# Two attention and two FFN layers on one core: FFN rows in homes of their own, spreads of 1/den by ScalarE and DMA

## The chip, the core and the metric
One core of one Trainium2 chip runs the whole program. The metric is the device time in microseconds of one launch. The engines are TensorE (PE in the rows, PEld for its weight loads), VectorE (DVE), ScalarE (ACT), GpSimd (POOL) and SyncE (SP), which here only issues DMAs.

## The reference
`x` has 2048 rows of 512 (bf16). Four residual layers follow each other, A, B, A, B, with the same weights both times (numbered L = 0 to 3):

```python
x = x + A(layernorm(x)); x = x + B(layernorm(x))   # twice
# A: 32 heads of 16
q, k, v = split(x @ wqkv)
phi = lambda t: where(t > 0, t + 1, exp(t)) + 1e-6
kv  = sum_s phi(k)[s] v[s]^T          # per head, 16 x 16
z   = sum_s phi(k)[s]
o   = (phi(q) @ kv) / (phi(q) . z + 1e-6)
A   = o @ wo
# B: 1792 hidden columns
B   = (silu(x @ w_gate) * (x @ w_up)) @ w_down
```

## The kernel before
The rows are 16 tiles of 128 (t), in 4 groups of 512 (g). The program is a list of tokens (`PROGRAM`, line 169) in the order in which TensorE does them; each token records its matmuls and all that belongs to it on the other engines. The order on the other four engines is written out by hand as well (`ORDER`, line 193), and `ON_ACT` (line 352) says which of two engines takes a step. Semaphore waits follow from the buffers that are read and written (`Prog.op`, `Prog.sync`). So a step runs when its turn has come on its engine and its inputs are there.

Tokens of an attention layer: `0k3` projects k of tile 3 and makes phi(k) (`k_proj`, line 663), `0g3` adds phi(k)^T x of tile 3 into four PSUM banks (`g_acc`; so kv is made from x first, and the weights of v come in later), `0z3` adds the sums z, `0q12` projects columns 2 of q for group 1 (`q_proj`), `0d12` makes the denominators of it (`den`, line 781), `0v` turns G into kv (`kvt`), `0m2` multiplies kv by Wo (`m_mm`), `0w5` is the output block of tile 5 with the residual (`wo`, line 854). The copies of G and of `0m` out of PSUM go to the buffer GT (`evac`, lines 741 and 744). `S` is a warming matmul on zeros.
Tokens of an FFN: `1u113` makes hidden columns 13 of group 1 (gate and up, `gu`, line 870), `1p25` is one of seven products of the down projection of group 2 (`down`, line 1101; a Winograd form of Strassen's scheme, so seven products instead of eight). In layer 3 some gate and up blocks are made by that scheme too (`3y...`, `gs`). `0t2` transposes a normed tile on TensorE (`xt_pe`, line 615).

`ln` (line 544) norms a tile: a sum (from the residual add, or for layer 0 by bn_stats on DVE or a copy with accumulation on ScalarE, line 564), a square with accumulation on ScalarE (line 572), variance and power -0.5 on DVE and POOL (lines 588, 592), and the apply on ScalarE (599) or DVE (603). Then SP transposes the tile by DMA into xnT (line 612), unless the token `t` does it. In attention layers the normed tile lies in xnA, one home per tile; in FFN layers in one of two buffers xnB that go round (line 553), and the square writes its unused output to one of three buffers etmp (line 568) that phi uses also.

1/den of a group has 32 numbers a row and has to be spread to 512. For 0d0, 0d1, 2d0 and 2d2 ScalarE takes a logarithm (line 797) and writes four spread tiles by an exponential (line 814) into one of two buffers rrep, SP transposes each, and DVE multiplies (line 832). For 0d3 and 2d3 DVE takes the reciprocal (803, 806) and ScalarE copies (819). For 0d2 and 2d1 (listed in `PE_T`) one exponential of 128 columns is transposed on DVE (808), TensorE spreads it by 16 small matmuls (`rep_pe`, line 834, token `0r2`), and DVE multiplies from PSUM (850).

## Time and profile before
| | us |
|---|---|
| median of 3 runs | 411.54 (411.19 to 414.91) |
| the profiled execution | 412.45 |
| its span | 410.5 |

The span is what the profile's rows cover; the execution's own time has 1.95 us around it. All times in rows are microseconds from the span's start. A group of rows names the line, the engine, the operation, the output and inputs, and the shape. In brackets stands how long the engine was idle before it and what ended that.

### The profile page before, as it was taken

What the parts mean: (1) busy time and instruction counts of PE and PEld (TensorE: products, weight loads), DVE (VectorE), ACT (ScalarE), POOL (GpSimd) and SP (SyncE); (2) the same over time, 40 slices, a digit from 0 to 9 for tenths busy, and PEclk for the clock granted to TensorE, in tenths of its full rate; (3) what the DMA queues carried; (4) which work ended last, traced back from release to release, by engine and by line L of the source; (5) the groups of instructions that cost most, each with busy time, mean ns of one, the idle gap of its engine ahead of it and who ended that gap; (6) DMA issues with size and microseconds to landing.
All of it is one profiled execution on the core that took longest, in us unless ns stands there. A gap on an engine that the chain in (4) does not pass through costs nothing.

```text
span 410.5 us, 7692 instructions
## 1 busy us (share of the span) xinstructions
PE 400.2 (97%) x2714; PEld 243.8 (59%) x2714; DVE 325.3 (79%) x754; ACT 245.9 (60%) x492; POOL 130.6 (32%) x277
## 2 busy tenths in 40 slices
...
PEclk9999999999999999999999999999999999999999
...
DMA packets 53190, 23.30 MB, mean 57 GB/s; under 512 B 46432, under 2 KB 52064, under 8 KB 53152
## 3 DMA queue, kind: packets, MB, share of 16 engines
...
q0 software_dynamic: 1344, 6.03, 4.6%
q10 hardware_dynamic: 544, 0.52, 0.4%
...
## 4 chain that ended last, share of the span: by engine, by line
PE 91%; DVE 4%; ACT 2%; DMA 1%; issue 1%; SPq 0%; DVEq 0%; ACTq 0%
PE pb L452 91%; DMA X<-in_A_x_dram 1%; DMA xnT<-xnB 1%; DVE X L862 1%; DVE pq L850 1%; DVE GT L744 0%; DVE pq L832 0%; ACT xnA L572 0%; ACT xnB L599 0%; ACT xnA L564 0%; DVE KVT L755 0%; DVE pq L659 0%; DVE pq L1205 0%; ACT xnT L631 0%; DVE etmp L652 0%
## 5 line engine op out<-in xcount | busy, mean ns | idle before, releaser
L452 PE MATMUL pb<-xnT,Wg 128*128 128x512 bf16 (+1 forms) x388 | 95.7, 363 | 1.4 <-issue 1.1
L452 PE MATMUL pb<-xnT,Wu 128*128 128x512 bf16 (+1 forms) x388 | 95.6, 363 | 0.0
L452 PEld LDWEIGHTS pb<-xnT,Wu 128*128 128x128 bf16 x388 | 37.9, 98 | 39.4
L452 PEld LDWEIGHTS pb<-xnT,Wg 128*128 128x128 bf16 x388 | 37.7, 98 | 36.1 <-issue 1.6
L896 DVE TENSOR_TENSOR hT<-tht,pb 128x512 bf16<-128x512 f32 x50 | 34.0, 682 | 22.0 <-PE pb L452 15.0
L894 ACT ACTIVATE tht<-pb 128x512 f32<-128x512 f32 x50 | 29.5, 592 | 27.9 <-PE pb L452 25.7
L647 ACT ACTIVATE etmp<-pb 128x512 bf16<-128x512 f32 x64 | 36.9, 597 | 12.1 <-PE pb L452 9.9
L1022 POOL TENSOR_TENSOR hT<-pq 128x256 bf16<-128x256 f32 x24 | 18.6, 778 | 77.2 <-ACT pq L1012 77.0
L576 POOL TENSOR_SCALAR mv<-sums 128x1 f32<-128x1 f32 x52 | 13.7, 271 | 87.4 <-DVE sums L1215 54.9
L885 ACT ACTIVATE tht<-pb 128x512 f32<-128x512 f32 x32 | 19.0, 595 | 35.5 <-PE pb L452 34.4
L452 PE MATMUL pb<-Wd,hT 128*128 128x256 bf16 x336 | 40.1, 273 | 0.0
L1027 ACT ACTIVATE pq<-pb 128x512 f32<-128x512 f32 x45 | 26.0, 595 | 22.6 <-PE pb L452 19.7
L592 POOL TENSOR_TENSOR rstd<-vpe,negh 128x1 f32<-128x1 f32 x62 | 35.9, 583 | 7.5 <-DVE sums L1215 2.7
L452 PEld LDWEIGHTS pb<-Wd,hT 128*128 128x128 bf16 x336 | 32.8, 98 | 5.8
L452 PE MATMUL pb<-Wqkv,xnT 128*128 128x512 bf16 x128 | 31.0, 379 | 2.4 <-ACT xnT L631 2.4
L1017 DVE TENSOR_TENSOR pq<-pb,pq 128x512 f32<-128x512 f32 x45 | 30.2, 684 | 3.6 <-PE pb L452 1.7
L452 PE MATMUL pb<-xnT,Wqkv 128*128 128x512 bf16 x128 | 31.9, 379 | 0.0
L452 PE MATMUL pb<-GT,pq 128*128 128x512 bf16 x128 | 30.2, 379 | 1.4 <-ACT GT L741 1.4
L452 PE MATMUL pb<-pk,xnA 128*128 128x512 bf16 x128 | 31.1, 379 | 0.0
L652 DVE TENSOR_SCALAR etmp<-etmp 128x512 bf16<-128x512 bf16 x64 | 18.3, 289 | 14.4 <-ACT etmp L647 14.2
L887 DVE SCALAR_TENSOR_TENSOR tht<-tht,pb 128x512 f32<-128x512 f32 x32 | 21.8, 684 | 6.2 <-ACT tht L885 6.0
L572 ACT ACTIVATE etmp<-X,sums 128x512 bf16<-128x512 bf16 x32 | 22.8, 714 | 3.9 <-DVE X L862 3.6
...
## 6 DMA issues: line engine op xcount, KB each, us to landing
...
```

Of the source, the lines that this page charges most:

```text
L452: return op("pe", lambda e: e.matmul(o_ap, lhsT=lhsT, rhs=rhs, start=start, stop=stop, skip_group_check=skip), r=r, w=w, n=n)
L572: op("act", lambda a: a.activation(out=sq_ap, in_=X[:, t, :], func=ACT.Square, scale=-float(D), bias=sums[:, t:t + 1], accum_out=mv[:, t, ...
L592: op("pool", lambda p: p.tensor_tensor(out=rstd[:, t:t + 1], in0=vpe[:, t:t + 1], in1=negh[:], op=ALU.pow), r=[f"vp{t}", "negh"], w=[f"rs{ ...
L647: exps.append(op("act", lambda a: a.activation(out=etmp[e][:], in_=PB[pb], func=ACT.Exp), r=[f"pb{pb}"], w=[f"e{e}"], after=silus, kind="e ...
L652: op("dve", lambda v: v.tensor_scalar(out=etmp[e][:], in0=etmp[e][:], scalar1=1.0, scalar2=1e-6, op0=ALU.min, op1=ALU.add), r=[f"e{e}"], w ...
L885: op("act", lambda e: e.activation(out=tht[a][:], in_=PB[pg], func=ACT.Tanh, scale=0.5), r=[f"pb{pg}"], w=[f"th{a}"], kind="tanh")
L887: op("dve", lambda v: v.scalar_tensor_tensor(out=tht[a][:], in0=tht[a][:], scalar=1.0, in1=PB[pg], op0=ALU.add, op1=ALU.mult), r=[f"pb{pg} ...
L894: silus.append(op("act", lambda e: e.activation(out=tht[a][:], in_=PB[pg], func=ACT.Silu), r=[f"pb{pg}"], w=[f"th{a}"], after=exps, kind=" ...
L896: op("dve", lambda v: v.tensor_tensor(out=hT[h][:, j, :], in0=tht[a][:], in1=PB[pu], op=ALU.mult), r=[f"pb{pu}", f"th{a}"], w=hk, kind="h")
L1017: op("dve", lambda v: v.tensor_tensor(out=c, in0=PB[b], in1=c, op=ALU.add), r=[f"pb{b}", k], w=[k], kind="ca")
L1022: lambda e: e.tensor_tensor(out=hT[h][:, jj, o:o + 256], in0=c[:, 0:256], in1=c[:, 256:512], op=ALU.mult),
L1027: op("act", lambda e: e.activation(out=gs_tmp[3 * f + n], in_=PB[pb], func=ACT.Copy), r=pk_, w=[f"gt{3 * f + n}"], kind="cp")
```

## The change
1. FFN rows: the normed tile of layers 1 and 3 goes to its own home, `pk[t]` for tiles 0 to 11 and `xnA[t]` for 12 to 15, and the square writes there as well. The ring xnB is gone.
2. Spreads: `PE_T` loses 0d2 and 2d1; all eight groups are now made by ScalarE's logarithm and exponentials and by DMA, 0d3 and 2d3 too. The ring rrep has four buffers. The small matrices for `rep_pe`, which ScalarE made at the start, are gone. `PE_T` gains 2t7.
3. Loads: the x tile 2 goes out on ScalarE's queue, between the two loads of k's weights.
4. The last group's third output block: the sum X + bank is made behind product 5, and the block is closed from that bank behind product 7.
5. The token list, the orders of the four engines and `ON_ACT` are all new. 31 warming matmuls stand ahead of tile 0's transposes instead of 51, and none behind them, where three stood.

The code (of the tables one line is shown):

```diff
 PE_T = set("""
-0d2 0t0 0t1 0t2 0t3 2d1
+0t0 0t1 0t2 0t3 2t7
 """.split())
...
         xnA = sb("xnA", [P, T, D // 2], FP32)[:].bitcast(BF16)
-        NXB = 2
-        xnB = [sb("xnB", [P, D], BF16) for _ in range(NXB)]
         NXT = 4
...
         esel = sb("esel", [P, H, DH], BF16) if any(x[1] == "d" for x in PE_T) else None
-        rrep = [sb("rrep", [P, 512], BF16) for _ in range(2)]
+        rrep = [sb("rrep", [P, 512], BF16) for _ in range(4)]
         RT = [sb("RT", [P, NC, 512], BF16) for _ in range(2)]
...
         r_pq = Ring(NPQ)
-        r_xb = Ring(NXB)
         r_xt = Ring(NXT)
         r_den = Ring(2)
-        r_rrep = Ring(2)
+        r_rrep = Ring(4)
         r_RT = Ring(2)
...
         for t in range(TG):
-            dma("sp", X[:, t, :], x2d[t * P:(t + 1) * P, :], w=[f"x{t}"], kind="ldx")
+            dma("act" if t == 2 else "sp", X[:, t, :], x2d[t * P:(t + 1) * P, :], w=[f"x{t}"], kind="ldx")
         for c in range(2):
...
             xk = f"x{t}"
-            if L % 2 == 0:
-                b_ap, bk = xnA[:, t, :], f"xa{t}"
-            else:
-                b = r_xb.take(1)
-                b_ap, bk = xnB[b][:], f"xb{b}"
+
+            b_ap, bk = (pk[t], f"pk{t}") if L % 2 and t < 12 else (xnA[:, t, :], f"xa{t}")
             if L == 0 and f"0s{t}" not in ON_ACT:
...
                        r=[xk], w=[bk, f"sm{t}"], kind="stats")
-                if L % 2:
-                    e = r_e.take()
-                    sq_ap, sqk = etmp[e][:], f"e{e}"
-                else:
-                    sq_ap, sqk = b_ap, bk
-                op("act", lambda a: a.activation(out=sq_ap, in_=X[:, t, :],
+                op("act", lambda a: a.activation(out=b_ap, in_=X[:, t, :],
                                                  func=ACT.Square, scale=-float(D), bias=sums[:, t:t + 1],
                                                  accum_out=mv[:, t, 1:2]),
-                   r=[xk, f"sm{t}"], w=[sqk, f"ss{t}"], kind="sq")
+                   r=[xk, f"sm{t}"], w=[bk, f"ss{t}"], kind="sq")
                 op("pool", lambda p: p.tensor_scalar(out=mv[:, t, 0:1], in0=sums[:, t:t + 1], scalar1=-1.0 / D,
...
                    r=[xk, f"mv{t}", f"rs{t}"], w=[bk], kind="apply")
-            if L % 2 and f"{L}t{t}" not in PE_T:
-                r_xb.done(b)
-            xn_of[L, t] = b_ap, bk, None if L % 2 == 0 else b
+            xn_of[L, t] = b_ap, bk
             if f"{L}t{t}" not in PE_T:
...
             dst = xnT[sl][:, :, tl * P:(tl + 1) * P]
-            b_ap, bk, xb = xn_of[L, t]
-            if xb is not None:
-                r_xb.done(xb)
+            b_ap, bk = xn_of[L, t]
             pb = bank()
...
             alone = last or f"{L}o{g}" in ON_ACT
-            assert done.issuperset({2: (1,), 6: (1,), 7: (6,), 4: (7,), 3: (5, 6) if alone else (5, 7)}.get(i, ()))
+            assert done.issuperset({2: (1,), 6: (1,), 7: (5, 6) if last else (6,), 4: (7,), 3: (5, 6) if alone else (5, 7)}.get(i, ()))
             f = i if i == 3 and alone or i == 4 and last else FIRST[i]
...
             if i == 7:
-                keep("c", pb, 2, hi_)
                 if last:
                     keep("e", pb, 2, lo_)
+                    ends(pbs, 2, hi_, "c")
                     pinned.discard(pb)
+                else:
+                    keep("c", pb, 2, hi_)
+            if i == 5 and last:
+                keep("c", pb, 2, hi_)
             if alone and i in (5, 6) and {5, 6} <= done:
...
                                                     in1=o_ap, op=ALU.add), r=[f"pb{d[5]}"] + ok, w=ok, kind="uu")
-            if i in (5, 7) and {5, 7} <= done:
+            if i in (5, 7) and {5, 7} <= done and not last:
                 ends([d[5]] * 2, 2, hi_, "c")
...
```

On TensorE the start of the program, before. `hT` is the tile of zeros of the warming matmuls, `ident,xnA` are transposes, `Wqkv,xnT` a projection of k (4 matmuls), `xnT,Wqkv` one of q, `pk,xnA` a step of G:

```order
L452 MATMUL pb<-hT 128x128 x51
L626 MATMUL pb<-ident,xnA 128x128 x4
L452 MATMUL pb<-hT 128x128
L452 MATMUL pb<-Wqkv,xnT 128x512 x4
L452 MATMUL pb<-hT 128x128 x2
L626 MATMUL pb<-ident,xnA 128x128 x12
L452 MATMUL pb<-Wqkv,xnT 128x512 x12
L452 MATMUL pb<-xnT,Wqkv 128x512 x8
L452 MATMUL pb<-pk,xnA 128x512 x16
```

The same place on TensorE now:

```order
L449 MATMUL pb<-hT 128x128 x31
L611 MATMUL pb<-ident,xnA 128x128 x4
L449 MATMUL pb<-Wqkv,xnT 128x512 x4
L611 MATMUL pb<-ident,xnA 128x128 x12
L449 MATMUL pb<-Wqkv,xnT 128x512 x12
L449 MATMUL pb<-xnT,Wqkv 128x512 x8
L449 MATMUL pb<-pk,xnA 128x512 x8
```

The real work up to q stands in the same order; 23 warming matmuls are gone.

On TensorE the first turn, before: copies into GT have begun, `Wo,KVT` are the products m, `GT,pq` the output blocks (4 matmuls each), `rT,esel` the spread by TensorE, `Zm,pq` denominators:

```order
L452 MATMUL pb<-Wo,KVT 128x512 x3
L452 MATMUL pb<-GT,pq 128x512 x12
L452 MATMUL pb<-Zm,pq 128x8 x4
L452 MATMUL pb<-rT,esel 128x128 x16
L452 MATMUL pb<-GT,pq 128x512 x8
L452 MATMUL pb<-xnT,Wqkv 128x512 x4
L452 MATMUL pb<-GT,pq 128x512 x4
L452 MATMUL pb<-Zm,pq 128x8 x4
L452 MATMUL pb<-GT,pq 128x512 x12
L452 MATMUL pb<-Zm,pq 128x8 x4
L452 MATMUL pb<-GT,pq 128x512 x12
L452 MATMUL pb<-xnT,Wg 128x512 x4
```

The first turn on TensorE now:

```order
L449 MATMUL pb<-Wo,KVT 128x512
L449 MATMUL pb<-GT,pq 128x512 x16
L449 MATMUL pb<-xnT,Wqkv 128x512 x4
L449 MATMUL pb<-GT,pq 128x512 x12
L449 MATMUL pb<-Zm,pq 128x8 x4
L449 MATMUL pb<-GT,pq 128x512 x16
L449 MATMUL pb<-Zm,pq 128x8 x8
L449 MATMUL pb<-GT,pq 128x512 x4
L449 MATMUL pb<-xnT,Wg 128x512 x4
```

The spread by TensorE is gone, and the tiles come as w3, w2, w0, w4, w1, w9, w5 and so on, where they came as w1, w2, w3, w0, w5, w4, w6.

On DVE the last steps, before. `pk` and `hT` are operand sums of the down products, `xnA<-pb,X` is X + bank, `pq<-pb,xnA` closes half a tile of the output:

```order
L1095 TENSOR_TENSOR pk<-hT,pk 128x1024
L1205 SCALAR_TENSOR_TENSOR pq<-pb,xnA 128x256
L1095 TENSOR_TENSOR pk<-hT,pk 128x768
L1139 TENSOR_TENSOR xnA<-pb,X 128x512
L1164 TENSOR_TENSOR xnA<-pb,xnA 128x512
L1205 SCALAR_TENSOR_TENSOR pq<-pb,xnA 128x256 x2
L1139 TENSOR_TENSOR xnA<-pb,X 128x512 x2
L1205 SCALAR_TENSOR_TENSOR pq<-pb,xnA 128x256 x4
```

The last steps on DVE now:

```order
L1080 TENSOR_TENSOR pk<-hT,pk 128x1024
L1124 TENSOR_TENSOR xnA<-pb,X 128x512
L1080 TENSOR_TENSOR pk<-hT,pk 128x768
L1194 SCALAR_TENSOR_TENSOR pq<-pb,xnA 128x256
L1124 TENSOR_TENSOR xnA<-pb,X 128x512
L1153 TENSOR_TENSOR xnA<-pb,xnA 128x512
L1194 SCALAR_TENSOR_TENSOR pq<-pb,xnA 128x256 x2
L1124 TENSOR_TENSOR xnA<-pb,X 128x512
L1194 SCALAR_TENSOR_TENSOR pq<-pb,xnA 128x256 x4
```

One of the two additions ahead of the last four closing steps has moved up, to between the last two operand sums.

## Rows read from the trace of the kernel before
**Rows 1.** The page: busy time by engine, and the granted clock in 40 slices.
```profile
PE 400.2 (97%) x2714; PEld 243.8 (59%) x2714; DVE 325.3 (79%) x754; ACT 245.9 (60%) x492; POOL 130.6 (32%) x277
...
PEclk9999999999999999999999999999999999999999
```
**Rows 2.** Timeline, first 12 us: start, length (us), instructions, idle before and what ended it.
```profile
3.04 0.69 DVE L557 BATCH_NORM_STATS2 stats<-X 128x6 f32<-128x512 bf16 x1 [1.86 <-DMA X<-in_A_x_dram]
...
4.34 0.63 ACT L564 ACTIVATE xnA<-X 128x512 bf16<-128x512 bf16 x1 [2.27 <-DMA X<-in_A_x_dram]
...
4.92 0.41 DVE L603 TENSOR_SCALAR xnA<-X,mv,rstd 128x512 bf16<-128x512 bf16 x1 [0.96 <-POOL rstd L592]
...
5.09 0.72 ACT L572 ACTIVATE xnA<-X,sums 128x512 bf16<-128x512 bf16 x1
...
5.47 0.39 PE L626 MATMUL pb<-ident,xnA 128*128 128x128 bf16 x4
...
6.03 0.69 DVE L557 BATCH_NORM_STATS2 stats<-X 128x6 f32<-128x512 bf16 x1 [0.70 <-DMA X<-in_A_x_dram]
...
7.90 1.04 PE L452 MATMUL pb<-Wqkv,xnT 128*128 128x512 bf16 x4 [1.99 <-ACT xnT L631]
...
10.12 2.76 PE L452 MATMUL pb<-Wqkv,xnT 128*128 128x512 bf16 x12 [0.40 <-ACT xnT L631]
```
**Rows 3.** Timeline of TensorE, 1.2 to 5.7 us: the warming matmuls.
```profile
1.25 4.39 PE L452 MATMUL pb<-hT 128*128 128x128 bf16 x51 [1.25 <-DVE hT L458]
...
3.35 0.94 PE L452 MATMUL pb<-hT 128*128 128x128 bf16 x7
...
4.18 0.83 PE L452 MATMUL pb<-hT 128*128 128x128 bf16 x12
```
**Rows 4.** Timeline, 55 to 70 us: the first turn from attention to FFN.
```profile
55.54 2.60 PE L452 MATMUL pb<-GT,pq 128*128 128x512 bf16 x11 [0.47 <-ACT GT L741]
...
58.15 0.40 PE L452 MATMUL pb<-rT,esel 32*128 32x128 bf16 x16
...
60.52 0.68 DVE L862 SCALAR_TENSOR_TENSOR X<-pb,X 128x512 bf16<-128x512 f32 x1
...
64.80 1.19 SPq L612 DMA_TRANSPOSE xnT<-xnB  x1
...
68.61 1.02 PE L452 MATMUL pb<-xnT,Wg 128*128 128x512 bf16 x4 [1.12 <-issue]
...
69.05 1.28 ACT L894 ACT_TABLE_LOAD   x1
```
**Rows 5.** DMA issues: count, and us from issue to landing.
```profile
xnT<-xnB SPq DMA_TRANSPOSE x32, 2.4
```
**Rows 6.** Timeline, 256 to 270 us: the second turn.
```profile
256.38 2.75 PE L452 MATMUL pb<-GT,pq 128*128 128x512 bf16 x12 [0.90 <-ACT GT L741]
...
269.32 1.04 PE L452 MATMUL pb<-xnT,Wg 128*128 128x512 bf16 x4 [0.29 <-DMA xnT<-xnB]
```
**Rows 7.** Stretches of the two turns: length, busy time of each engine.
```profile
56.00:68.70 12.70, 11.58 (x79) 5.36 (x79) 12.56 (x37) 11.17 (x25) 7.63 (x23) 1.00 0.38 63
...
257.00:270.00 13.00, 12.71 (x74) 5.81 (x73) 13.00 (x38) 11.84 (x28) 9.83 (x26) 1.00 0.35 71
```
**Rows 8.** Groups by line: count, busy us, mean ns, idle before.
```profile
L832 DVE TENSOR_TENSOR pq<-pq,RT 128x512 bf16<-128x512 bf16 x24 | 11.0, 471 | 2.9 <-DMA RT<-rrep 2.8
...
L850 DVE TENSOR_TENSOR pq<-pq,pb 128x512 bf16<-128x512 bf16 x8 | 5.4, 675 | 0.0
...
L814 ACT ACTIVATE rrep<-dsb 128x512 bf16<-128x512 f32 x16 | 9.7, 634 | 4.0 <-DMA RT<-rrep 4.0
```
**Rows 9.** Timeline, the last 6 us.
```profile
405.14 1.69 PE L452 MATMUL pb<-Td,hT 128*128 128x256 bf16 x14
...
405.34 1.29 DVE L1139 TENSOR_TENSOR xnA<-pb,X 128x512 f32<-128x512 f32 x2 [0.70 <-PE pb L452]
...
406.55 1.40 DVE L1205 SCALAR_TENSOR_TENSOR pq<-pb,xnA 128x256 bf16<-128x256 f32 x4
```

More of the change, by code (lines that the diff above doesn't have):

```diff
@@ L191 @@
+3y335 3y336 3p21 3y332 3y322 3y327 3p26 3y337 3p22 3p27 3y324 3y323 3y341 3y333 3u313 3y346 3p24 3y345 3y347 3y342
+3p23 3y334 3y343 3y344 3p31 3p32 3p35 3p36 3p33 3p37 3p34
 """
@@ new lines @@
+2q21.exp 2q21.id1 2q03.exp 2q13.exp 2q20.exp 2d0.ln 2q20.id1 2d0.rex 2d0.rex3 2d0.rex2 2q23.exp 2q23.id1 2d0.rex1
+2q22.id1 2q22.exp 2d1.ln 2d1.rex 2d1.rex3 2d1.rex2 2d2.ln 2G0.evac 2G3.evac 2d1.rex1 2q33.exp 2q33.id1 2d2.rex
+2M1.evac 2M0.evac 2M2.evac 2d2.rex2 2d2.rex3 2d2.rex1 3x3.sq 3x2.sq 2q32.exp 2q32.id1 3x0.sq 3x1.sq 3x6.sq
+3x0.apply 2q30.exp 3x1.apply 3x5.sq 3x4.sq 3x8.sq 2d3.ln 3x10.sq 2d3.rex 2d3.rex3 2d3.rex2 2d3.rex1 3x7.sq
+3u011.silu 3u012.silu 3u008.silu 3x11.sq 3x7.apply 3u002.silu 3x9.sq 3x11.apply 3u005.silu 3x13.sq 3u000.silu
@@ new lines @@
+3u009.silu 3u003.silu 3x12.sq 3x8.apply 3u004.silu 3x13.apply 3x14.sq 3u010.silu 3x15.sq 3y101.cp 3u006.silu
+3x12.apply 3u007.silu 3y111.cp 3y106.cp 3y102.sih 3y112.sih 3u001.silu 3x15.apply 3u112.silu 3y107.cp 3y116.cp
+3u013.silu 3y107.sih 3y117.cp 3y104.sih 3y117.sih 3y121.cp 3y103.sih 3y114.sih 3y113.sih 3y131.cp 3y126.cp 3y136.cp
+3u106.silu 3y132.sih 3y137.cp 3y127.cp 3y122.sih 3u113.silu 3y137.sih 3y127.sih 3y134.sih 3y124.sih 3y123.sih
+3u105.silu 3y141.cp 3y133.sih 3y211.cp 3u206.silu 3u212.silu 3y146.cp 3y216.cp 3y147.cp 3y217.cp 3y142.sih
@@ new lines @@
+1x8.vpe Wd.tw2 1u001.h 1u000.h Wd.tw 1u002.h Wd.tw5 1u012.h 1u007.h Wd.tw6 1u003.h 1x8.apply 1u113.h 0d3.pqn2
+0d3.pqn1 1u109.h 1u013.h 0d3.pqn 0d3.pqn3 1u100.h Wd.tw3 1u004.h Wd.tw4 1u010.h Wd.tw1 1u006.h 0w14.res 1x14.vpe
+1u104.h 1u101.h 0w13.res 1u110.h 1u111.h 1u009.h 1h0.sb 1h0.sa 1u106.h 1h0.sb1 0w12.res 1h0.sa1 1h0.sa3 1u103.h
+0w15.res 1h0.sb3 1x12.vpe 1h0.sb2 1p01.uu 1x12.apply 1h0.sa2 1u108.h 1x15.vpe 1u107.h 1p06.uu 1u112.h 1p07.uu
+1p07.rh 1p07.rh1 1u102.h 1h1.sb 1h1.sb3 1u105.h 1h1.sa 1p03.rh 1p03.rh1 1h1.sb1 1h1.sa3 1p02.rh1 1p02.rh 2x0.tot
@@ new lines @@
+2x11.vpe 1h3.sa3 1p23.rh1 2x11.apply 1h3.sb2 1p31.uu 1h3.sa2 2x8.tot 1p23.rh 1p24.tot 1p23.tot 2x9.vpe 1p36.uu
+2k7.ts 1p36.uu1 2k7.phi 2k7.zs 1p33.rh1 1p33.rh 2k1.ts 2k1.phi 2k11.ts 2k11.phi 1p37.uu 1p37.rh 1p37.rh1 2q02.ts
+2q02.phi 2k9.ts 2k9.phi 1p34.rh1 1p34.rh 2x14.tot 1p34.tot 1p32.rh1 1p32.rh 2x15.vpe 2x12.tot 1p32.tot 2x14.vpe
+2x15.apply 2k10.ts 2k10.phi 2x14.apply 2k10.zs 2x12.apply 2x13.apply 2q00.ts 2q00.phi 2q12.ts 2q12.phi 2k8.ts
+2k8.phi 2q11.ts 2q11.phi 2k15.ts 2k15.phi 2k12.ts 2k15.zs 2k12.phi 2k12.zs 2k13.ts 2k13.phi 2q31.ts 2q31.phi
@@ new lines @@
+2d3.pqn1 3u012.h 3u008.h 2d3.pqn2 2d3.pqn 3u002.h 2w13.res 2d3.pqn3 gsw.ws 3x10.apply 3u005.h 3gx1.xs1 3u000.h
+3x9.apply 3u009.h 3gx1.xs 3u003.h 2w12.res 3gx1.xs2 2w14.res gsw.ws2 gsw.ws7 3u004.h 2w15.res gsw.ws5 gsw.ws8
+3u010.h gsw.ws6 gsw.ws10 3u006.h 3u007.h 3y102.ca 3y112.ca 3y112.hp 3u001.h 3h0.sb 3x14.apply 3h0.sb3 3u112.h
+3y107.ca 3u013.h 3h0.sa 3y117.ca 3h0.sb1 3y104.hh 3h0.sa1 3p01.uu 3h0.sa3 3y103.ca 3h0.sb2 3y103.hp 3h0.sa2
+3y113.ca 3y114.hh 3y117.hp 3p06.uu 3y113.hp 3p07.uu 3p07.rh1 3p07.rh 3u106.h 3p03.rh 3p03.rh1 3y132.ca 3y132.hp
```

275 lines of the change are left out of this document (124 added, 151 removed).

## The prediction, made before the change was run
> **What bounds the kernel now.** I read the page's busy shares first: TensorE is busy 97% of the span and the granted clock is full in every slice [rows 1]. So only three things can move the time: TensorE's own work, the few places where it waits, and what lies before its first and behind its last matmul. I then looked in the timeline for TensorE rows with an idle time ahead of them. They lie in three places. At the start, the first projection of k waits 1.99 us for a copy out of PSUM and the next three 0.40 [rows 2]. At the turn from the first attention to the first FFN, the first output row block waits 0.47 for the copies of GT and the first gate matmul 1.12 [rows 4]. At the turn from the second attention to the second FFN it is 0.90 and 0.29 [rows 6]. These add to 5.17 us. Between and behind the turns TensorE runs on without a wait worth a row. The end is DVE: the last matmuls start at 405.14, DVE is done at 407.95 (406.55 + 1.40), and the span ends at 410.5 [rows 9]. Everything that the change could win is therefore some 6 us of 411, if all of these went.
>
> **The start.** Tile 0 is now summed on ScalarE instead of DVE. From rows 2: the tile is there at 3.04; sum 0.75 (4.34 to 5.09) and square 0.82 (0.72 and the read of the sum) give 4.61; from the end of the statistics to DVE's apply it is 1.19 now (3.73 to 4.92); without the step that aggregates I put 0.9, so the apply starts at about 5.5 where it stood at 4.92, and the transposes at about 6.05 instead of 5.47. But the copy out of PSUM now stands on DVE right behind the applies of tiles 0 and 1, where before it stood on ScalarE behind the sums and squares of tiles 2 and 3 (the wait of 1.99). I get 7.1 for the first k instead of 7.90: 0.8 earlier. Tile 1, which was fourth on SP's queue and came at 6.03, is now second and no longer last; tile 2 goes out on ScalarE's queue, between its two weight loads, at about the same 1.3.
> The other three k's don't get that gain. Tiles 2 and 3 are applied on DVE behind the statistics of tiles 4 and 5 (0.69 each, the price of the row at 3.04): 7.1 + 2 x 0.69 + 2 x 0.41 and 0.5 for small steps makes 9.8, then TensorE transposes them (in order, ahead of the next k), and the next k starts at about 10.1; it stood at 10.12. So of 0.8 I keep 0.1. Bounds: -0.8 if ScalarE and DVE get to tiles 2 and 3 earlier than I chain them, +0.9 if the copy of tile 2, which stands on ScalarE behind five other steps, lets a k (4 x 0.22) wait. I take **-0.1**.
>
> **The first turn.** Spreading 1/den by TensorE is gone for groups 0d2 and 2d1: 16 small matmuls each, 0.33 us (the 0.40 of the row at 58.15, less the drain of the last) [rows 4]; DVE loses four multiplies that read PSUM (0.68 each) for four that read a transposed tile (0.47 as the mean) [rows 8], and a transpose. ScalarE gets four exponentials over 512 columns (0.63) [rows 8] for one over 128, and SP four more transposes, ahead of the first FFN rows on its queue; one holds the queue 1.19 [rows 4] and lands in 2.4 [rows 5]. With four buffers for the spreads instead of two, ScalarE no longer waits for a transfer (4.0 us in all [rows 8]). Chained by these prices, ScalarE's last copy of GT ends where it does now, within 0.3: two of four copies go to DVE, but three more spreads stand ahead. That wait I leave as it is.
> What moves is the order of the output blocks. Before, block 0 came fourth, behind the 16 small matmuls; its sum stood on DVE behind two PSUM multiplies and started at 60.52, its transposed tile was issued at 64.80 and released the gate matmul at 68.61 [rows 4], 8.1 us after the sum. That last tile landed 3.8 after its issue, against 2.4 as the median [rows 5], which I put down to the transpose issued just ahead of it, still under way. Now block 1 is the last, one position later (w3, w2, w0, w4, q, w1). Its sum starts at about 61.3, but its square, power and apply have no ring of two xnB tiles to wait for, and by my chain the tile ahead of it is issued a good 1.5 earlier; I get an issue at 65.1 and a landing at 67.5 to 68.1. TensorE itself has 12 output blocks and one q, 13 x 0.86, and 0.3 of denominators to do from 55.6, and is there at 67.1. So the gate starts at about 67.7 instead of 68.61. I take **-0.9**, the 0.33 included. Bounds: -1.5 (TensorE alone sets the start) and +0.5 (the landing takes 3.8 again from an issue at 65.3).
> FFN rows in homes of their own also free the squares from the etmp ring; inside the turn this is in the chain above, and outside it nothing waits. One thing is new: all of 0d3 is now made by ScalarE ahead of the first SiLU (a logarithm, four exponentials of 0.63), where it was two DVE steps and copies in the middle of the FFN. ScalarE loads its table at 69.05 today [rows 4]; I get 71.0. TensorE can do four column blocks (8 x 0.22 each) in the eight banks before it needs that SiLU, up to 74.6, and the first banks come free at about 73.6: hidden by 1 us, and up to 1 us lost if that cover goes.
>
> **The body, the second turn, the end.** One tile of layer 2 (2t7) is transposed on TensorE instead of by DMA: 4 matmuls, 0.22 (0.39 less the 0.17 in which one drains, row at 5.47): **+0.2**. A reordered body will have a few waits that the old one didn't: I take **+0.3**, bounds 0 and 1.2 (what one turn has today).
> At the second turn the order of the blocks is the same as before. ScalarE reaches its copies of GT at the same time, so the 0.90 stays. The 0.33 of small matmuls go, and DVE, which has no idle time there [rows 7], loses 4 x 0.21 and a transpose but gets one more addition of weight sums ahead of block 1. The gate should follow TensorE's last output block with less than the 0.29 of now [rows 6]: **-0.5**, bounds -0.8 and +0.6.
> At the end the sum X + bank for the third output block's half is made at 3p35, a step earlier, and the block is closed at 3p37. DVE then has one add of 0.61 instead of two between 405.34 and the four closing writes [rows 9]: 405.34 + 0.61 + 4 x 0.35 = 407.35, where 407.95 is now. But that add now stands ahead of the sum that 3p33 reads, and I expect 0.25 of delay there. **-0.35**, bounds -0.6 (all of it) and +0.1.
> Sum: -0.1 - 0.9 + 0.2 + 0.3 - 0.5 - 0.35 = -1.35 us. The profiled execution took 412.45 (span 410.5 and 1.95 around it), which would become 411.1; it lies 0.9 above the median of the runs, 411.54, and I carry the difference to the median: **410.2 us**. The bounds together give 407.7 to 415.
>
> **Rivals.**
> *The clock.* Only 31 warming matmuls are left of 51 ahead of tile 0. Before, they started at 1.25 with a spacing of 0.105 ((0.94 - 0.31) / 6), and from about 4.2 of 0.055 ((0.83 - 0.22) / 11): 1.2 GHz, then 2.4 [rows 3]. 28 fit before 4.2, so 31 end at about 4.4, 0.2 us behind the rise, where the old ones went on to 5.64. Then TensorE has only four transposes until 7.1. If the clock doesn't rise, or falls again, k matmuls of 0.22 take 0.43. Four k's (16 matmuls) cost up to 3.4; I take 12 matmuls, 2.6, for -1.35 + 2.6 = +1.25: 412.8, at most 413.7. From 1.35 us on, that is about 6 matmuls at the lower clock, the change makes the kernel slower. Against it: today's pause of two microseconds ahead of 7.90 left the clock up, since the four k matmuls there took 0.22 each [rows 2].
> The Trainium skill, "TensorE: Matmul & The Clock Gate", Part 1, says that "the default state is throttled, and activity releases the throttle"; the halved spacing agrees with it. Part 4 of the page says that transposes on TensorE don't count as activity in the same way, which would speak for this rival; no run here shows it.
> *Nothing gained at the turns.* ScalarE and DVE are both nearly full there [rows 7], and the transposes share one queue with eight more spreads; then the tiles come no earlier and only the 0.66 of small matmuls and the end remain against 0.5 in the body: 411.3.
> *More than I chain.* The start keeps 0.7 and the first turn all of its 1.5: -2.8, 408.7. For it speaks that nearly all rings and waits of the turn are loosened at once; against it, that DVE stays full.
>
> **How the numbers follow.** Forecast 0.50, nothing gained 0.20, the clock 0.17, more 0.13. The range 407.9 to 413.7 reaches to the last two rivals; about 2 in 10 are left out for waits that I don't see. Faster or slower by over 1% (4.1 us, about what a measurement of this kernel can tell from no change) needs 407.4 or 415.7: all my cases lie between, and beyond them I leave 0.08 and 0.06.
>
> **What would show it.** Right: first k near 7.1 but the second near 10.1; gate of the first FFN at about 67.5, of the second at about 268 less the shift; DVE's last add alone at the end. Wrong: k matmuls at 0.43 spacing, TensorE waiting for a SiLU near 74, a landing above 3.5 for block 1's tile, or new waits of over a microsecond in the body.

## The result: 1.1% slower, and where the profile after puts it

The changed kernel takes 415.97 us (median of 12 runs, 414.42 to 420.96), the kernel before 411.83 beside it: a ratio of 1.0113, 95% interval 1.0091 to 1.0136. Medians here and below are over all executions, ratios over those within 1.5% of the fastest of their kernel, so the two need not divide out. Forecast were 410.2 and a range to 413.7; the measured time lies outside. The profiled execution took 417.38, its span 415.6 where it was 410.5.

To see where, I cut both spans at five rows of TensorE's timeline: the first accumulation of G (`pb<-pk,xnA`), the first matmul of KVT (`pb<-GT,Wqkv`), the first FFN gate matmul (`xnT,Wg`), and the last two again in layers 2 and 3. Lengths in us:

| stretch | before | after | difference |
|---|---|---|---|
| start to first G step | 14.44 | 15.93 | +1.49 |
| to KVT | 36.73 | 40.02 | +3.29 |
| to the first gate matmul (first turn) | 17.44 | 17.81 | +0.37 |
| to KVT of layer 2 (body) | 184.18 | 184.75 | +0.57 |
| to the second gate matmul (second turn) | 16.53 | 16.52 | -0.01 |
| to the end | 141.18 | 140.57 | -0.61 |

The page of the kernel after, its first two parts; they answer to [rows 1]. TensorE's busy time is 1.3 us longer, and one slice, the sixth (52 to 62 us), no longer has the full clock:

```profile
PE 401.5 (97%) x2622; PEld 244.3 (59%) x2663; DVE 327.2 (79%) x754; ACT 243.0 (58%) x495; POOL 132.3 (32%) x267
...
PEclk9999989999999999999999999999999999999999
```

**The start.** Timeline of TensorE and VectorE, against [rows 2, 3]:

```profile
1.24 3.49 PE L449 MATMUL pb<-hT 128*128 128x128 bf16 x31 [1.24 <-DVE hT L455]
6.00 0.60 PE L611 MATMUL pb<-ident,xnA 128*128 128x128 bf16 x4 [1.28 <-DVE xnA L592]
7.22 1.89 PE L449 MATMUL pb<-Wqkv,xnT 128*128 128x512 bf16 x4 [0.61 <-DVE vpe L577]
7.95 0.69 DVE L551 BATCH_NORM_STATS2 stats<-X 128x6 f32<-128x512 bf16 x1 [0.73 <-DMA X<-in_A_x_dram]
...
9.29 0.70 DVE L592 TENSOR_SCALAR xnA<-X,mv,rstd 128x512 bf16<-128x512 bf16 x2
...
10.98 3.38 PE L449 MATMUL pb<-Wqkv,xnT 128*128 128x512 bf16 x11 [0.22 <-ACT pk L635]
...
15.93 1.24 PE L449 MATMUL pb<-pk,xnA 128*128 128x512 bf16 x5
```

The 31 warming matmuls end at 4.73, TensorE idles 1.28 us, and the first four k matmuls, at 7.22 as forecast, take 1.89 us where four took 1.04: half the speed. The granted clock in the profile does not show this: it reads 1.00 from 7.2 to 9.0 us. The run with more warming matmuls below, where they take 1.04, speaks for the clock all the same. The next eleven take 3.38.

**To KVT.** The lines that decide are not among those I had read before. Wo's load and the eight gate/up loads go out on GpSimd's queue when the last x tile of layer 0 has been transposed. GpSimd's issues, kernel before, then kernel after:

```profile
31.15 0.98 POOL L495 DMA_DIRECT2D Wo<-in_A_wo_dram  x1 [4.62 <-DMA xnT<-xnA]
...
41.95 0.54 POOL L495 DMA_DIRECT2D Wg<-in_B_w_gate_dram  x1 [0.58 <-DMA Wu<-in_B_w_up_dram]
```

```profile
34.69 0.98 POOL L492 DMA_DIRECT2D Wo<-in_A_wo_dram  x1 [8.46 <-DMA xnT<-xnA]
...
45.65 0.54 POOL L492 DMA_DIRECT2D Wu<-in_B_w_up_dram  x1 [0.60 <-DMA Wg<-in_B_w_gate_dram]
```

They are 3.5 us later, from the first to the last (3.7). The change sums x tiles 11 and 12 on ScalarE, which comes to them late. That is the smaller part, some 0.4 us: with these sums back on VectorE (below) Wo's load goes out at 33.25, and in two runs that leave them on ScalarE and start about as early (first G step at 14.91 and 14.96 against 14.79) at 33.66 and 33.71. The rest comes with the later start and the other new orders. Tile RT, to which SP's transposes write the spreads, kernel before and after (duration of the issues, idle time of the reader, us from issue to landing):

```profile
L823 SPq DMA_TRANSPOSE RT<-rrep x8: 1188/1190/1216, 43.5 to 58.3; - x8
...
  DMA RT<-rrep: 1.7, 1
...
DMA to landing us min/median/max: 2.4/2.4/3.7
```

```profile
L808 SPq DMA_TRANSPOSE RT<-rrep x12: 1188/1193/2361, 45.5 to 64.3; - x12
...
  DMA RT<-rrep: 4.4, 2
...
DMA to landing us min/median/max: 2.4/2.4/6.7
```

The first spread goes out at 45.5 us in the kernel after, while the last loads are still arriving; a transfer that lands in 2.4 us took up to 6.7. What follows from it, timeline of the kernel after:

```profile
52.32 0.84 DVE L817 TENSOR_TENSOR pq<-pq,RT 128x512 bf16<-128x512 bf16 x2 [3.67 <-DMA RT<-rrep]
...
52.73 0.63 ACT L799 ACTIVATE rrep<-dsb 128x512 bf16<-128x512 f32 x1 [2.22 <-DMA RT<-rrep]
...
54.15 0.26 PE L449 MATMUL pb<-Zm,pq 128*128 128x8 bf16 x4 [1.30 <-DVE pq L644]
54.79 0.63 ACT L799 ACTIVATE rrep<-dsb 128x512 bf16<-128x512 f32 x1 [1.42 <-DMA RT<-rrep]
...
55.13 1.28 DVE L729 CAST GT<-pb 128x512 bf16<-128x512 f32 x2
55.32 1.06 ACT L726 ACTIVATE GT<-pb 128x512 bf16<-128x512 f32 x2
...
55.95 0.28 PE L449 MATMUL pb<-GT,Wqkv 128*128 128x128 bf16 x2 [1.55 <-ACT GT L726]
...
57.45 1.91 PE L449 MATMUL pb<-xnT,Wqkv 128*128 128x512 bf16 x4
...
61.85 0.59 ACT L726 ACTIVATE GT<-pb 128x512 bf16<-128x512 f32 x1
```

VectorE waits 3.67 us for the first spread, ScalarE 2.22 and 1.42 for a free buffer. Behind them in the queues stand the last phi(q) of group 2 and the copies of G (ScalarE's at 55.32, VectorE's at 55.13), so TensorE waits 1.30 and 1.55 us ahead of KVT. After that pause its matmuls run at half clock (four in 1.91). Here the granted clock shows it; stretch of 2 us, with length, busy time of TensorE, weight loads, VectorE, ScalarE and GpSimd, clock, DMA share, GB/s:

```profile
57.40:59.40 2.00, 1.96 (x7) 0.78 (x6) 1.64 (x5) 1.29 (x4) 0.00 (x0) 0.50 0.33 66
```

Two microseconds at 0.50 are, by my estimate, 1 us of the first turn's stretch.

**Body, second turn, end**, against [rows 6, 9]; the x transposes of layer 2, the second turn, the last matmuls and VectorE's last rows:

```profile
236.37 1.04 PE L449 MATMUL pb<-Wqkv,xnT 128*128 128x512 bf16 x4 [0.29 <-DMA xnT<-xnA]
...
261.62 2.82 PE L449 MATMUL pb<-GT,pq 128*128 128x512 bf16 x11 [0.53 <-ACT GT L726]
...
273.02 0.26 PE L449 MATMUL pb<-Zm,pq 128*128 128x8 bf16 x4 [0.61 <-DVE pq L644]
...
410.88 1.69 PE L449 MATMUL pb<-Td,hT 128*128 128x256 bf16 x14
...
411.69 1.41 DVE L1194 SCALAR_TENSOR_TENSOR pq<-pb,xnA 128x256 bf16<-128x256 f32 x4
```

### The profile page after: what moved, and what is told of

Same layout as the page of the kernel before. It is cut to its first block, busy times and chain, and to the rows that moved or that the text cites. A ratio compares the mean times of both kernels' runs of the same rounds, so it can differ in the third digit from the quotient of the medians.

```text
span 415.6 us, 7550 instructions
## 1 busy us (share of the span) xinstructions
PE 401.5 (97%) x2622; PEld 244.3 (59%) x2663; DVE 327.2 (79%) x754; ACT 243.0 (58%) x495; POOL 132.3 (32%) x267
## 4 chain that ended last, share of the span: by engine, by line
PE 82%; DVE 6%; DMA 5%; ACT 4%; issue 2%; SPq 1%; POOL 0%; DVEq 0%; ACTq 0%
PE pb L449 82%; DMA RT<-rrep 4%; ACT rrep L799 1%; SPq L808 1%; DMA X<-in_A_x_dram 1%; DVE pk L1080 1%; DVE xnA L1124 1%; DMA xnT<-xnA 1%; ACT pq L635 1%; ACT etmp L632 1%; DVE pq L1194 1%; ACT L472 0%; DVE pq L817 0%; DVE etmp L637 0%; DVE pk L644 0%
## 5 line engine op out<-in xcount | busy, mean ns | idle before, releaser
L449 PE MATMUL pb<-xnT,Wg 128*128 128x512 bf16 (+1 forms) x373 | 92.7, 362 | 0.8
L881 DVE TENSOR_TENSOR hT<-tht,pb 128x512 bf16<-128x512 f32 x54 | 36.6, 684 | 25.3 <-PE pb L449 19.2
L1007 POOL TENSOR_TENSOR hT<-pq 128x256 bf16<-128x256 f32 x19 | 14.0, 740 | 80.5 <-ACT pq L997 77.6
L565 POOL TENSOR_SCALAR mv<-sums 128x1 f32<-128x1 f32 x56 | 15.8, 285 | 71.9 <-DVE X L847 37.7
L581 POOL TENSOR_TENSOR rstd<-vpe,negh 128x1 f32<-128x1 f32 x61 | 35.4, 588 | 10.1 <-DVE vpe L577 5.7
L561 ACT ACTIVATE xnA<-X,sums 128x512 bf16<-128x512 bf16 x32 | 22.8, 715 | 22.1 <-DVE sums L1204 15.9
L449 PE MATMUL pb<-Wqkv,xnT 128*128 128x512 bf16 x121 | 32.6, 395 | 1.8 <-DVE vpe L577 0.6
L637 DVE TENSOR_SCALAR etmp<-etmp 128x512 bf16<-128x512 bf16 x64 | 19.6, 307 | 14.6 <-ACT etmp L632 14.3
L997 ACT ACTIVATE pq<-pq 128x256 f32<-128x256 f32 x45 | 18.4, 414 | 16.2 <-DVE pq L1002 15.9
```

The source lines that it names most:

```text
L449: return op("pe", lambda e: e.matmul(o_ap, lhsT=lhsT, rhs=rhs, start=start, stop=stop, skip_group_check=skip), r=r, w=w, n=n)
L561: op("act", lambda a: a.activation(out=b_ap, in_=X[:, t, :], func=ACT.Square, scale=-float(D), bias=sums[:, t:t + 1], accum_out=mv[:, t, 1 ...
L565: op("pool", lambda p: p.tensor_scalar(out=mv[:, t, 0:1], in0=sums[:, t:t + 1], scalar1=-1.0 / D, scalar2=None, op0=ALU.mult), r=[f"sm{t}" ...
L581: op("pool", lambda p: p.tensor_tensor(out=rstd[:, t:t + 1], in0=vpe[:, t:t + 1], in1=negh[:], op=ALU.pow), r=[f"vp{t}", "negh"], w=[f"rs{ ...
L637: op("dve", lambda v: v.tensor_scalar(out=etmp[e][:], in0=etmp[e][:], scalar1=1.0, scalar2=1e-6, op0=ALU.min, op1=ALU.add), r=[f"e{e}"], w ...
L881: op("dve", lambda v: v.tensor_tensor(out=hT[h][:, j, :], in0=tht[a][:], in1=PB[pu], op=ALU.mult), r=[f"pb{pu}", f"th{a}"], w=hk, kind="h")
```

## The experiments

All ratios are to the kernel before on the same chip. My theory after reading the traces was that the late loads cost the 3.3 us; rivals were the low clock at the start, the order in which the copies of G stand behind the spreads, and the third group's spreads, which are new on the queue.

**Three single edits and all three.** More warming matmuls:

```diff
-S x31 0t0 0k0 0t1 0t2
+S x54 0t0 S S S S 0k0 S S 0t1 0t2
```


> The changed kernel with 54 warming matmuls ahead of the first transposes and six between them and the first k products, in place of 31 and none. If the cold start costs the 1.5 us by which the first G step comes late (15.93 against 14.44 us), the first k products run at 0.22 us a matmul from the start, the first G step comes at about 14.5 us and the whole takes about 414.5 us. If instead the x tiles' loads and the norms on VectorE and ScalarE hold the start (waits of 0.73, 0.54 and 0.49 us for x), the clock is high but the first G step stays near 15.9 us and the time near 416. Neither theory lets this run touch the wait ahead of KVT, which should stay some 4 us behind that of the kernel before, less what the start gives.

The copies of G and masks of KVT ahead of the spreads (ScalarE shown, VectorE alike):

```diff
-0q20.exp 0d1.ln 0d1.rex1 0d1.rex3 0G0.evac 0G3.evac 0d1.rex2
+0q20.exp 0d1.ln 0G0.evac 0G3.evac 0d1.rex1 0d1.rex3 0d1.rex2
```


> The changed kernel with the copies of G (and the masked copies of KVT) ahead of the spreads and of the multiplications by them on ScalarE and VectorE. If the order in those two queues is what makes TensorE wait (1.30, 1.55 and 0.23 us ahead of and in KVT, with the clock lost after it), KVT begins at about 52.7 us in place of 55.95, no stretch at half clock follows, and the time is about 413 us. If the late transposes of the spreads are the cause whatever stands behind them, KVT comes early but the same 3 us are lost behind it, at the first output tiles of Wo that need a normed phi(q), and the time stays at 415 to 416.

The sums of tiles 11 and 12 back on VectorE (with their places in the orders of ScalarE, VectorE and GpSimd):

```diff
 ON_ACT:
-0r14 0s0 0s11 0s12 0s13
+0r14 0s0 0s13
```


> The changed kernel with the sums of x tiles 11 and 12 back on VectorE (bn_stats), so that the last transposed x tile is issued earlier, and with it the nine weight loads that wait for it. If those loads, 3.5 us later than before, delay the spreads' transposes (up to 8.5 us to landing, 3.7 before), then the last x transpose is issued at about 28 in place of 31.6 us, the last gate/up load at about 42 in place of 45.65, the spreads land within 4 to 5 us, KVT begins near 53 us and the time is about 413. If only the order of copies and spreads counts, or the third group's spreads by DMA, KVT stays near 55.9 and the time near 416.

And all three:

> The three edits together: more warming matmuls, copies of G ahead of the spreads, sums of tiles 11 and 12 on VectorE. If the start and the collision ahead of KVT are the whole loss, the first FFN gate matmul comes at 68.5 to 69.5 us in place of 73.8 and the time is 411 to 412, the kernel before's. If a third cause is hidden (the middle and the tail), it stays at 413 or above though the first FFN gate matmul is back at 69.

Measured: warming 415.79 (ratio 1.0093, 1.0065 to 1.0121), copies 417.03 (1.0119, 1.0079 to 1.0160), sums 412.05 (0.9999, 0.9978 to 1.0019), all three 413.28 (1.0035, 1.0017 to 1.0053). The sums alone give back the whole loss. All three together met the second case of what I expected: the first FFN gate matmul is back at 69.21, and the time is 1.2 us above that of the sums alone. The warming did what it was to do at the start; timeline of TensorE and VectorE:

```profile
7.17 1.04 PE L449 MATMUL pb<-Wqkv,xnT 128*128 128x512 bf16 x4 [0.30 <-DVE xnT L619]
...
9.31 0.71 DVE L592 TENSOR_SCALAR xnA<-X,mv,rstd 128x512 bf16<-128x512 bf16 x2
...
10.31 2.75 PE L449 MATMUL pb<-Wqkv,xnT 128*128 128x512 bf16 x12
...
14.63 1.89 PE L449 MATMUL pb<-pk,xnA 128*128 128x512 bf16 x8
```

The first G step is back at 14.63, and the time is not: the stretch to KVT still took 39.02 us. With the copies first that stretch fell to 36.88 us, so the order of the queues can take this wait away; but in the same execution the body and the second turn were each 1 us longer than in the kernel before (185.45 and 17.50), and the other three executions took 2 to 4 us more than the profiled one. Why, I have not found; the order theory promised 413 and fell with its time.

**Is it the loads?** The sums also take two sums and two squares off ScalarE, about 0.8 us each by the rows of tile 0 [rows 2], so the loads were tried without them. The eight gate/up loads behind the second group's spreads:

```diff
-for w_ in weights:
-    w_(last)
+weights[0](last)
...
+if len(rts) == 8 and weights:
+    for w_ in weights[1:]:
+        w_(rts[4:])
```


> The changed kernel with the eight gate/up loads (not Wo's) made to wait for the second group's four spread transposes in place of the layer-0 x transposes, so that they cannot lie under the first two groups' spreads; the late sums of tiles 11 and 12 stay. If the loads under the spreads are the cause, the spreads land in 2.4 to 4 us, VectorE's wait of 3.7 us for the first of them goes, KVT begins at about 52 us and the time is 412 to 414 (the FFN may now wait for its last weights, up to 2 us). If the late sums cost the time in another way, KVT stays at 54 to 56 us and the time at 416.

Without the third group's spreads:

```diff
-for tl in range(TG):
+for tl in range(0 if (L, g) == (0, 2) else TG):
```


> The changed kernel without the third token group's spreads in layer 0: its four exponentials, four transposes and four multiplications are left out, so that group's phi(q) goes into Wo without its 1/den. If the third group's spreads by DMA, new in the change, are what costs, the time falls to about 412. If the loads under the first group's spreads are the cause, KVT is as late as before (54 to 56 us) and the time falls by no more than the 1 to 2 us of VectorE and ScalarE work that is missing behind it, to about 415.

The kernel before with late loads:

```diff
-w_(last)
+w_(last + exps[-1:])    # called behind token 0q11
```


> The kernel before, with one thing alone: Wo's and the eight gate/up loads also wait for the exponential of the second column block of phi(q) of group 1, which ends at about 34.4 us, so that they start some 3.3 us later, as in the changed kernel. If loads under the spreads cost the time, its first spread transposes land in 6 to 8 us in place of 2.4 to 3.7, KVT begins 2 to 4 us later than 51.2 us, and the time is 413.5 to 415.5. If the loads' lateness is harmless, the time stays at 411.5.

> The changed kernel with the sums of tiles 11 and 12 on VectorE and the longer warming, without the edit that put the copies of G first. If the low clock at the start costs over 1 us by itself, it takes about 411 us. If the start's clock costs little (the first G step came at 14.79 us with the short warming and at 14.80 with the long one), it stays at 412, like the sums alone, and the 1.2 us by which the three edits together were slower than the sums alone belong to the copies' order.

Measured: loads held back 423.10 (1.0275, 1.0245 to 1.0305); without the third spreads 415.72 (1.0079, 1.0048 to 1.0110); before with late loads 418.83 (1.0118, 1.0067 to 1.0170); sums and warming 414.85 (1.0076, 1.0054 to 1.0098). Late loads alone make the kernel before as slow as the changed one, and leaving the third group's spreads out brings the ratio from 1.0113 to 1.0079 only, as expected if they are not the cause: that rival is out. In the kernel before with late loads the direction was as expected and the sizes were not: KVT came 1.4 us later than in the kernel before, not 2 to 4, and the time lies above the 415.5 I had put as the most; the profiled execution (414.77) is one of its two fastest. Tile RT in the kernel before with late loads, 4.8 us of waiting where it was 1.7:

```profile
  DMA RT<-rrep: 4.8, 3
...
  ACT rrep L814: 4.8, 1
...
DMA to landing us min/median/max: 2.4/2.5/5.9
```

Held back, the loads let the stretch to KVT shrink to 36.96 us, the value of before, as expected; but I had put the price behind it at 2 us, and it was 9. The loads now run from 58.7 us on, tile RT has a landing of 9.1 us, and the last phi(q) stands on VectorE behind the multiplications that wait for it. Timeline of TensorE:

```profile
72.53 0.27 PE L449 MATMUL pb<-Zm,pq 128*128 128x8 bf16 x4 [8.15 <-DVE pq L641]
```

The last run was a miss: the warming on top of the sums costs. The stretch from 45 to 52 us, sums alone and sums with warming (columns as above), shows that the sums alone had not cleared the loads away either:

```profile
45.00:52.00 7.00, 7.00 (x63) 3.60 (x60) 2.94 (x8) 5.13 (x11) 0.00 (x0) 1.00 0.87 193
```

```profile
45.00:52.00 7.00, 7.00 (x58) 3.53 (x56) 1.91 (x6) 4.40 (x9) 0.00 (x0) 1.00 1.17 192
```

With the sums alone the last load goes out 0.7 us ahead of the first spread (43.92 and 44.62), where it was 0.1 behind (45.65 and 45.54); with warming besides it is 1.7 ahead (43.17 and 44.83). Among the first three groups' spreads the slowest landed in 5.0 and 5.8 us, and VectorE waited 1.9 us for them with the sums alone, where it was 4.4. So the moment of the loads does not tell these two runs apart. Between the profiled spans lie 1.6 us: 0.3 at the start, 0.5 in the stretch to KVT, 0.6 in the second turn. Why the warming costs is open.

**Two more ways round.** The norms of tiles 7, 8, 11 and 12 earlier as well; two loads held back; both:

```diff
 sp:
-0x7.xT 0x12.xT 0x8.xT 0x11.xT
+0x8.xT 0x7.xT 0x12.xT 0x11.xT
```


> The changed kernel with the sums of tiles 11 and 12 on VectorE as in the earlier run, and besides the norms of tiles 7, 8, 11 and 12 a few places earlier on ScalarE and VectorE, tile 8's transpose ahead of tile 7's. Nothing else is changed. If the time follows the moment at which the gate/up loads are done against the first spreads, the first load starts at about 32 us (33.25 with the sums alone, 31.15 in the kernel before), the spreads land within 5 us and the time is 410.5 to 411.5, at or below the kernel before. If the loads' moment is not what counts, it stays at 412 like the sums alone.

```diff
-i.ld i.ld6 i.ld7 i.ld3 i.ld5 i.ld2 i.ld4 i.ld1 i.ld8
+i.ld i.ld5 i.ld6 i.ld2 i.ld4 i.ld1 i.ld3 j.ld j.ld1    # j: after the second group's spreads
```


> The changed kernel with one thing alone: the last two of the eight gate/up loads wait for the second group's spread transposes, so that six run ahead of the spreads and two behind them; the late sums of tiles 11 and 12 stay. If the collision is the cause, KVT begins near 53 us (52.7 with all eight held back, 55.95 in the changed kernel), the FFN has its weights in time, and the time is 412 to 413. If six loads still lie under the first spreads (the sixth would be issued at about 43.5 us, the first spread at 45.5), the gain is half of that, 414.

> Both: the earlier norms and sums, and the last two loads held back until the second group's spreads have landed. If the collision is the whole loss of the change, what is left is the change's own gain at the turns and the end (some 1 us by the profile of the sums alone: 0.6 at the first turn, 0.25 at the second, 0.5 at the end, less 0.26 in the body), and the time is 410 to 411, under the kernel before. If the two loads held back delay the third group's spreads or the FFN, it is 412 or more.

Measured: 413.93 (1.0052, 1.0030 to 1.0074), 417.71 (1.0142, 1.0103 to 1.0182), 416.65 (1.0125, 1.0087 to 1.0162): the first two expectations of the time missed, the third came out by its worse case (412 or more). In the first the loads were out of the way (the spreads landed in 2.5 us as the median, the slowest in 4.1), but my new order of the norms made TensorE wait 1.78 us for a phi(k) at 27 us. Of the two loads held back, the stretch to KVT tells the same as above (36.97 us), but they fell upon the third group's spreads, and the first turn took 21.19 us.

**The moment of the loads alone.** So the loads must come between the last x transposes and the first spreads. The shortest edit that moves them, and nothing else, lets them start two transposes earlier:

```diff
-last = list(xT_of.values())
+last = [o for (_, t), o in xT_of.items() if t not in (8, 11)]
```


> The changed kernel with one thing alone: Wo's and the gate/up loads no longer wait for the last two layer-0 transposes (tiles 8 and 11), so they start some 2.5 us earlier, at about 32 in place of 34.7 us. If the moment of the loads is the cause, the stretch from the first G step to KVT falls from 40.0 to 37 or 38 us and the time to 412.5 to 414. If the sums of tiles 11 and 12 cost in another way (ScalarE's and VectorE's own work around 20 to 29 us), it stays at 416.

> The changed kernel with the sums of tiles 11 and 12 on VectorE and the loads freed of the last two transposes. Loads start at about 30.7 us in place of 33.25 with the sums alone. By the loads' moment, G to KVT takes at most 37 us in every execution, no execution shows a lower clock, and the time is 410.5 to 411.5, under the 412.05 of the sums alone. If the two transposes that now lie beside Wo's load are late for their k products (needed some 3 us later), TensorE waits near 36 us and the time is 412 to 414.

In the kernel before, whose last two are 11 and 12:

> The kernel before with its loads freed of the last two layer-0 transposes, so that they start 1.3 to 2.5 us earlier than 31.15 us. By the loads' moment its spreads land in 2.4 us each where the slowest took 3.7, which had cost TensorE nothing: the time stays at 411.3 to 411.6, or gains 0.2 at most. If earlier loads cost by themselves (by delaying the last transposes), it is slower, 412 to 413.

And with the norms of tiles 2 and 3 first on VectorE:

> As the sums with freed loads, and on VectorE the norms of tiles 2 and 3 ahead of the statistics of tiles 4 and 5 (which wait 0.6 to 0.7 us for their loads), so that the second to fourth k products come about 1 us earlier. If the start then counts, the first G step comes at 13.8 to 14.2 us in place of 14.8 to 16.9, and the time is 409.5 to 410.5, below both kernels. If an earlier start only runs into the loads again (as the longer warming did), G to KVT grows by what the start gives and the time stays as without it.

Measured: one line in the changed kernel 411.87 (1.0013, 0.9994 to 1.0031); with the sums 412.12 (1.0017, 1.0003 to 1.0031); the kernel before 411.30 (0.9980, 0.9942 to 1.0018); with the start 412.03 (1.0008, 0.9988 to 1.0028). The one line gives back 4.1 us, more than I had put on it. The sums and the start add nothing to it, though I had expected at most 411.5 and 410.5 with them; with the new start the first G step came at 14.96, not by 14.2. GpSimd's first issue in the kernel with the one line alone, and its tile RT:

```profile
31.95 0.98 POOL L492 DMA_DIRECT2D Wo<-in_A_wo_dram  x1 [5.94 <-DMA xnT<-xnA]
```

```profile
  DMA RT<-rrep: 1.2, 2
...
DMA to landing us min/median/max: 2.4/2.5/4.1
```

The stretch from 45 to 52 us in that kernel, and then in the kernel after:

```profile
45.00:52.00 7.00, 7.00 (x56) 3.45 (x55) 3.84 (x9) 5.55 (x12) 0.00 (x0) 1.00 0.52 123
```

```profile
45.00:52.00 7.00, 6.95 (x55) 3.46 (x54) 0.72 (x2) 4.16 (x8) 0.59 (x2) 1.00 1.04 257
```

While the first spreads are under way the DMA engines are busy 0.52 of the time instead of all of it, and VectorE works 3.84 us in it instead of 0.72. Six of the kernels with the changed body line up with this, one profiled execution each. Last load 0.1 us behind the first spread (the kernel after): 40.0 us to KVT. Ahead by 0.2 (without the third spreads) or 0.3 (warming): 39.1 and 39.0. By 0.7 (sums) or 1.7 (sums and warming): 37.1 and 37.7. By 2.4 (the one line): 36.7. The order isn't perfect, but it fits that the sums alone undid the loss: with them the loads start 0.8 us earlier against the spreads, and 2.9 of the 3.3 us are gone.

The Trainium skill, "DMA: Bandwidth & Descriptors", section "Issuing engines are not separate DMA queues", says that transfers issued by different engines run on the same 16 DMA engines and interleave. The trace agrees: the loads are on GpSimd's queue, the spreads on SP's, and a spread's landing went from 2.4 to 6.7 us.

**What is left, and the other edge.** With the loads put right the start is still 1.3 us late. Warming with 46, then the norms of tiles 2 and 3 first, then one transpose less to wait for:

> The changed kernel with the loads freed of the last two transposes and 46 warming matmuls ahead of the first transposes and six behind them, in place of 31 and none. If the lower clock makes the start late, the first four k matmuls take 1.04 us (1.89 now), the first G step comes at 14.4 to 14.9 us in place of 15.71 and the time is 410.7 to 411.2, against 411.87 without the warming. If the order on VectorE does, the time stays at 411.9.

> The same and, on VectorE, the norms of tiles 2 and 3 ahead of the statistics of tiles 4 and 5, which wait for their loads. By the order on VectorE the second k comes at about 9.3 us in place of 10.3, the first G step at 13.8 to 14.2, and the time is 410 to 410.5. If VectorE only shifts its lateness to the later tiles (its work is the same), the first G step stays at 14.5 to 15 and the time is that of the run without it.

> The same and the loads freed of tile 12's transpose too, so that they start some 1.3 us earlier again, at about 30.5 us. If an earlier start of TensorE brings the first spreads back under the last loads, this run is faster than the one with two transposes freed, by up to 1 us (409.5 to 410); if they are clear of each other already, it is the same; if the freed transposes land late for their k products, it is slower by 0.5 to 1.5.

Measured: 412.88 (1.0017, 1.0004 to 1.0031), 413.72 (1.0032, 1.0018 to 1.0047), 420.95 (1.0211, 1.0175 to 1.0247). With the clock up, the first k's take 1.04 us, but the next transposes wait for VectorE; with VectorE's order changed they come at 9.0 and 9.6, and a later copy is waited for instead. Timeline of TensorE, warming alone, then with the new order:

```profile
7.27 1.04 PE L449 MATMUL pb<-Wqkv,xnT 128*128 128x512 bf16 x4 [0.59 <-DVE xnT L619]
...
10.19 0.72 PE L611 MATMUL pb<-ident,xnA 128*128 128x128 bf16 x8 [1.55 <-DVE xnA L592]
...
15.28 1.89 PE L449 MATMUL pb<-pk,xnA 128*128 128x512 bf16 x8
```

```profile
9.56 0.40 PE L605 MATMUL pb<-ident,xnA 128*128 128x128 bf16 x4 [0.21 <-DVE xnA L586]
...
11.28 2.06 PE L443 MATMUL pb<-Wqkv,xnT 128*128 128x512 bf16 x8 [0.46 <-DVE xnT L613]
```

Neither made the kernel faster, and none of the 18 runs beats the kernel before by more than its interval. The third shows the other edge of the gap for the loads: three transposes early, the last x tiles land under them, in 7.8 and 8.2 us. I had put 0.5 to 1.5 us on that; against the run with two transposes freed it costs 7.

```profile
40.31 1.84 PE L443 MATMUL pb<-xnT,Wqkv 128*128 128x512 bf16 x4 [4.17 <-DMA xnT<-xnA]
```

## Why the prediction was wrong

With the loads freed by one line, the stretches of the changed kernel are 15.71, 36.69, 16.32, 184.76, 16.38 and 140.54 us: against the kernel before +1.27, -0.04, -1.12, +0.58, -0.15 and -0.64, together -0.1. Against these I hold my terms.

*The first turn (-0.9).* Here the step fails on which everything hung: "ScalarE's last copy of GT ends where it does now, within 0.3". It ended at 55.97 before (54.88 + 1.09) and at 62.44 after (61.85 + 0.59, shown above). I had chained the spreads with 2.4 us each from the kernel before and asked only what they cost their own queue. I did not ask what the later norms, those of tiles 11 and 12 among them, release: the last x transpose, and through it nine loads. The prediction never names those loads. With them freed the copy ends at 57.08, 4.7 us behind the start of KVT where it was 4.8: apart from the loads and the late start, this chain held. ScalarE, kernel before, then the changed kernel with its loads freed:

```profile
54.88 1.09 ACT L741 ACTIVATE GT<-pb 128x512 bf16<-128x512 f32 x2
```

```profile
56.44 0.64 ACT L726 ACTIVATE GT<-pb 128x512 bf16<-128x512 f32 x1
```

The turn itself is then 1.12 shorter; but the kernel before with its loads freed has almost the same turn, 16.26, and no wait ahead of its gate matmul (TensorE, 67.48). So the 1.12 of wait that I meant to win [rows 4] is not won by the new order of the blocks. Nor had the loads caused it: in the kernel before the last of them was issued at 41.95, and the slowest of them took 7.3 us to land, so all were done 15 us earlier. It hung on one transpose. The landing of the two x tiles issued at 63.5 and 64.8, kernel before, then with its loads freed:

```profile
DMA to landing us min/median/max: 2.4/3.0/3.6
```

```profile
DMA to landing us min/median/max: 2.4/2.4/2.4
...
67.48 1.02 PE L452 MATMUL pb<-xnT,Wg 128*128 128x512 bf16 x4
```

Both have the same transpose just ahead, so my reason for the long landing falls too; what made it long I don't know. The profiled spans (410.5 and 409.3) differ by what the turns differ, 1.2. The kernel before with its loads freed took 411.2 to 411.3 in seven of ten executions, 412.4 to 412.7 in three. That fits a wait which comes in some executions only, though no trace shows it for the others. If so, the median to which I carried the gain had little of that wait left to give.

*The start (-0.1).* First k at 7.22 against 7.1: right. The second at 10.98 against 10.1, the first G step 1.49 late: wrong. The speed of TensorE, which I had as a rival, did fall. The 31 warming matmuls kept a spacing of 0.106 to their end ((3.49 - 0.31) / 30), so the rise that I had put at 4.2 us did not come within them. In ten profiled executions with 31 warming matmuls and the change's order on VectorE the first G step came at 14.79 to 16.87 us (median 15.7), in four with more of them at 14.63 to 15.28 (14.9): by these medians the clock costs about 0.8. But where it was put right the time did not follow, so as the cause of the result this rival falls. In the step itself little was wrong: VectorE had applied tiles 2 and 3 by 9.99 (9.29 + 0.70), 0.2 behind my 9.8. I had taken the loads of tiles 4 and 5, whose statistics stand ahead, as landing when they did in the kernel before, and VectorE waited 0.73 for the first (the median of the 256 KB loads of x went from 4.7 to 7.5 us). With 54 warming matmuls the tiles were applied by 10.02, no earlier, and yet the second k came at 10.31: most of its 0.9 of lateness goes with the clock.

*The body (+0.2 and +0.3).* +0.57: 2t7's four transposes of 0.22 and one wait of 0.29 for a transposed tile at 236 us. The cover of 1 us ahead of the first SiLU held: TensorE has no wait there.

*The second turn (-0.5).* Nothing gained. The wait for the copies of GT, which I had left at 0.90, fell to 0.53, but the last phi(q) now stands on VectorE behind output blocks, and TensorE waits 0.61 for it at 273 us: a new wait in the place of the old.

*The end (-0.35).* -0.61: right, a little more. VectorE ends 2.22 us behind the start of the last matmuls (410.88), 2.81 before.

The rival *nothing gained at the turns* comes nearest for the turns; no rival had the mechanism of the loss, and my 0.06 for slower by over 1% was all I gave it. Three of my sums don't come out of their terms: the bounds together begin at 408.0 and not 407.7, *nothing gained* gives 411.0 or 410.9 and not 411.3, *more than I chain* 409.0 and not 408.7. None of them touches the forecast or the step that failed.
